# An attention and MLP kernel whose whole schedule is a printed list: the list replaced, with VectorE's squares and statistics kept apart from GpSimd's array reads

## The chip, the cores and the metric

The kernel runs on one core of a Trainium2 chip. The metric is the device time of one execution in microseconds; the time of the kernel before is the median of three runs. Beside these there is one profiled execution, with a record of every instruction: its time is 166.68 us, its span (first to last recorded instruction) 165.0 us.

## The reference, cut to what matters

Sparse attention over 4 batches of 8 heads (768 tokens, head size 64), each query seeing the 8 first tokens and its 96 last ones, with a bias that grows with distance; then, on the 3072 tokens of width 512, a projection to 1024, a SoLU with a layer norm, and a projection back.

```python
scores = scale * np.matmul(q, k.transpose(0, 1, 3, 2)) + bias
scores = np.where(keep, scores, -1000000000.0)     # 8 global tokens, 96 local ones
a = softmax(scores)
x = np.matmul(a, v)                                # (B, H, S, D) -> (B*S, H*D)
h = x @ w_in
solu = h * softmax(h)
mu = np.mean(solu, axis=-1, keepdims=True)
var = np.mean((solu - mu) ** 2, axis=-1, keepdims=True)
out = ((solu - mu) / np.sqrt(var + 1e-06) * g_ln) @ w_out
```

## The kernel before

All work is cut into 1116 steps; 762 of them issue something or hold a buffer and stand in a list, the others are landings of transfers and releases of buffers. A step is a handful of instructions on one engine. The kernel builds the steps in a fixed order (so each has a number), and then emits them in the order of the list `ORDER`. `SLOTS` says which buffer each step takes, `ENGS` which engine runs a step that could run on several, and `WARM` where matmuls on a constant (L1215) are put in between, only to keep TensorE at work. Each engine runs its steps in the order of the list and waits, at each, for what that step needs; a step that waits holds up everything behind it on its engine. SP is the queue that issues nearly all transfers, and it too goes strictly by the list: a load whose buffer isn't free yet holds up the loads behind it.

The steps of one batch b, with its head pairs p = 0 to 3:

- loads of q and k (384 KB each, into 7 buffers x32), a cast to 16 bits with a reordering (L271, L273, L275, on ScalarE, VectorE or GpSimd), 6 transposes on TensorE (L712) and a copy out of PSUM ("evac", L271 or L273). For batch 0 v comes in parts of 96 and 64 KB, later in parts of 192 and 160 KB, into 3 buffers v32, and is cast by any of the three.
- on GpSimd four small products on k for the global tokens (kg, L515); on TensorE the scores in two groups of columns for each pair (L839, L854), and the global scores (L910, L916); on ScalarE their exponentials (L862, L923). For batches 1 to 3 VectorE multiplies a factor on (fac, L871), which makes the bias; its table fb is made at the start (L314, L320).
- in two units u of 384 tokens: row sums on TensorE (L937, L946), their logarithm on ScalarE (L953), a split of it into a high part (lhi, L960, one buffer) and a rest (l16, a subtraction, L968) on VectorE or GpSimd, a spreading to all rows on TensorE (L997), the reciprocal as an exponential on ScalarE (L1006), probabilities times v on TensorE (av1, av2, L1031, L1041, with a one-column copy, "tick", L1051, between them), and their product on VectorE (xT, L1066).
- for each of 24 tiles t of 128 tokens: the first projection (gemm1, L1104; for tiles 0 to 5 in two halves), its exponential with row sums on ScalarE (ef, L1114), the product on VectorE (u, L1117, which frees the projection's pair of PSUM banks), the square with its row sum on ScalarE (L1124) or VectorE (L1128), a transposition by the DMA engines (tiles 5 to 21, issued by SP, L1133, into the buffer "late") or by TensorE (L1143), the output matmul (gemm2, L1189), its scaling (osb, L1199 on ScalarE, L1202 on VectorE) and the store (L1206).
- for each group of three tiles, four instructions on VectorE that make the variance from the row sums (stats, L1160 to L1167; groups are numbered 0 to 7), and two on ScalarE for its inverse root (L1171, L1172).

Once, at the start: constants on GpSimd and VectorE, among them iota (L297 to L301), the identity and a scaled identity (L289, L290), the bias (L338), and the slopes (L370); w_in and w_out, each as four loads of 512 KB; eight casts of w_in (four for each half of the columns); a mean over w_out (L626 part_mean, a copy on ScalarE, L631) and its centring on VectorE (L634, 8 steps), which the output matmul needs.

A step is given a mark `port` if its name begins with one of the names in `PORT`. The mark isn't read anywhere in the kernel.

Of the kernel before, what the change touches and what calls it, by code (L numbers as in the profile page):

```python
# [29 lines left out]
FACT = {1, 2, 3}  # L30
SPLIT = False
ORDER = """
# [32 lines left out]
"""  # L65
SLOTS = """
# [11 lines left out]
"""  # L78
ENGS = """
# [4 lines left out]
"""  # L84
WARM = """
28:0:4 34:0:1 44:4:1 51:4:1 78:2:4 97:6:2 113:4:3 120:4:2 145:2:3 173:6:1 199:5:1 203:4:1
"""


PORT = ("cast_", "w_in_cast", "c_far", "c_bias", "c_local", "c_rows", "fac", "lhi", "l16", "c_gbc",  # L90
        "c_spread", "c_sumg", "kg", "vgz")


class Plan:
# [1159 lines left out]
```

## Time and profile before

| | |
|---|---|
| median of 3 runs | 167.39 us (165.78 to 167.76) |
| profiled execution | 166.68 us, span 165.0 us |
| TensorE's granted clock | 1.00 in all stages |
| TensorE matmul instructions | 1955 |
| bytes moved by DMA | 34.26 MB, mean 208 GB/s |

The profile is read in five ways here. A table gives each engine's busy time over the span. A table by stretches gives the length, the busy time of TensorE's matmuls, of its weight loads, of VectorE (DVE), ScalarE (ACT) and GpSimd (POOL), each with the number of instructions, then the granted clock, the mean busy share of the 16 DMA engines, and GB/s. The timeline of an engine gives start, duration, engine, line, operation, output and input, and in brackets the idle time before it with what ended it; equal instructions in a row are merged (x5), and SPq is SP's issuing queue. A table of groups gives the instructions of one line with their total, their mean in ns, and the idle time before them. Names like acc (PSUM) or x are the program's tile names without buffer numbers.

### The profile page before, as it was taken

To read this page: it belongs to the slowest core of one execution; us is meant where nothing else is said; L and a number is where in the kernel's file an instruction comes from. 1 tells how busy PE (TensorE), PEld (TensorE's weight loads), DVE (VectorE), ACT (ScalarE), POOL (GpSimd) and SP (SyncE) were. 2 spreads that over 40 slices of the span, in tenths; PEclk is the share of its full clock that TensorE was granted. 3 is DMA by queue.
4 is the path that set the end of the run, shared out by engine and by line. 5 is a ranking of instruction groups with operands and counts; after the bars stand their busy time and mean duration, and the time that the engine had idled before them with its cause. 6 is when DMAs were issued, how large, how long until landed. Compare 5 with 4: busy or idle time off the path is not lost.

```text
span 165.0 us, 4929 instructions
## 1 busy us (share of the span) xinstructions
PE 148.6 (90%) x1955; PEld 82.1 (50%) x1955; DVE 128.1 (78%) x270; ACT 124.6 (76%) x206; POOL 52.3 (32%) x121
## 2 busy tenths in 40 slices
PE   4498976998998999989999999999997899997991
PEld 1366544345656655556555444574443464443650
DVE  6978334889987999989899999387979565569850
ACT  3566957659999999997999799787985752866612
POOL 7774515367166456443450610120041000000000
PEclk9999999999999999999999999999999999999999
DMA  4999699999999989899966449940672831359333
GB/s 153 372 346 258 159 321 359 392 339 275 293 299 301 292 224 228 231 285 336 297 111 133 100 92 264 265 171 0 131 120 72 189 124 71 71 128 123 124 134 126
DMA packets 58390, 34.26 MB, mean 208 GB/s; under 512 B 44920, under 2 KB 53376, under 8 KB 58368
## 3 DMA queue, kind: packets, MB, share of 16 engines
q1 hardware_dynamic: 57360, 32.26, 72.1%
q10 hardware_dynamic: 1008, 1.70, 3.0%
q8 instruction: 15, 0.25, 0.7%
q14 instruction: 7, 0.06, 0.1%
HBM read 23.20 MB, written 6.29 MB: 179 GB/s over the span
## 4 chain that ended last, share of the span: by engine, by line
PE 46%; DVE 18%; ACT 10%; DMA 8%; POOL 6%; issue 6%; SPq 2%; ACTq 0%; POOLq 0%; DVEq 0%
PE acc L1189 17%; PE acc L1104 10%; DVE uu L1117 6%; DMA v<-in_v_dram 5%; PE acc L1041 4%; PE acc L712 4%; ACT eb L862 3%; DMA late<-uu 3%; DVE gw_out_sb L634 2%; ACT ef L1114 2%; DVE eb L871 2%; DVE xT L1066 2%; PE acc L997 2%; DVE sqv L1128 2%; PE acc L1143 2%
## 5 line engine op out<-in xcount | busy, mean ns | idle before, releaser
L1189 PE MATMUL acc<-gw_out_sb,late 128*128 128x512 f16 (+1 forms) x200 | 44.7, 371 | 0.8 <-DMA late<-uu 0.8
L1104 PE MATMUL acc<-w_in_sb,xT 128*128 128x512 f16 x192 | 44.3, 379 | 0.5 <-DVE uu L1117 0.4
L1117 DVE SCALAR_TENSOR_TENSOR uu<-ef,acc 128x1024 f16<-128x1024 f16 x24 | 29.1, 1218 | 7.6 <-ACT ef L1114 7.3
L862 ACT ACTIVATE eb<-acc 128x960 f16<-128x960 f32 (+1 forms) x32 | 29.0, 949 | 4.9 <-PE acc L854 4.7
L1114 ACT ACTIVATE ef<-acc 128x1024 f16<-128x1024 f32 x24 | 24.7, 1030 | 9.7 <-PE acc L1104 9.6
L1189 PEld LDWEIGHTS <-late 128*128 128x128 f16 x200 | 18.6, 98 | 21.0 <-DMA late<-uu 1.3
L1104 PEld LDWEIGHTS <-xT 128*128 128x128 f16 x192 | 18.1, 98 | 21.8 <-issue 1.8
L1066 DVE TENSOR_TENSOR xT<-acc,rr 128x384 f16<-128x384 f32 x32 | 16.2, 551 | 4.5 <-PE acc L1041 2.4
L871 DVE TENSOR_TENSOR eb<-eb,fb 128x960 f16<-128x960 f16 x24 | 16.6, 697 | 3.3 <-ACT eb L862 3.1
L275 POOL CAST x<-x 128x768 f16<-128x768 f32 x17 | 15.6, 928 | 10.1 <-DMA x<-in_k_dram 3.1
L712 PE MATMUL acc<-ident,x 128*128 128x128 f16 x192 | 15.8, 231 | 2.9 <-ACT x L271 1.6
L712 PEld LDWEIGHTS <-x 128*128 128x128 f16 x192 | 12.7, 104 | 8.7 <-ACT x L271 2.9
L1006 ACT ACTIVATE rr<-acc 128x768 f32<-128x768 f32 x16 | 12.6, 809 | 5.3 <-PE acc L997 4.4
L1041 PE MATMUL acc<-eb,v 64*64 64x160 f16 (+4 forms) x448 | 14.8, 219 | 1.7 <-ACT lns L953 0.9
L1124 ACT ACTIVATE sqa<-uu 128x1024 f16<-128x1024 f16 x14 | 14.9, 1066 | 0.5 <-ACT osb L1199 0.4
L1041 PEld LDWEIGHTS <-v 64*64 64x64 f16 x448 | 12.6, 106 | 4.4 <-issue 2.9
L275 POOL CAST v<-v 128x704 f16<-128x704 f32 (+3 forms) x14 | 7.8, 582 | 21.0 <-DMA v<-in_v_dram 19.9
L1199 ACT ACTIVATE osb<-acc,rstd 128x512 f32<-128x512 f32 (+1 forms) x16 | 10.4, 672 | 4.4 <-PE acc L1189 4.1
L1128 DVE SCALAR_TENSOR_TENSOR sqv<-uu 128x1024 f16<-128x1024 f16 x10 | 12.6, 1260 | 0.1
L854 PE MATMUL acc<-qT,kT 64*64 64x160 f16 (+2 forms) x384 | 11.8, 230 | 0.5 <-ACT eb L862 0.5
L968 POOL TENSOR_TENSOR l<-lns,lhi 128x384 f16<-128x384 f32 x5 | 6.7, 1331 | 16.3 <-DVE lhi L960 15.6
L273 DVE COPY kT<-acc 128x768 f16<-128x768 f16 x11 | 10.5, 952 | 1.4 <-PE acc L712 1.4
(116 smaller groups left out, 206.3 us busy)
## 6 DMA issues: line engine op xcount, KB each, us to landing
x<-in_q_dram SPq DMA_DIRECT2D x16, 384.0 KB, 5.0
x<-in_k_dram SPq DMA_DIRECT2D x16, 384.0 KB, 6.4
out_dram<-osb SPq DMA_DIRECT2D x17, 256.0 KB, 4.0
v<-in_v_dram SPq DMA_DIRECT2D x12, 192.0 KB, 4.8
w_out<-in_moe_w_out_dram SPq DMA_DIRECT2D x4, 512.0 KB, 6.0
late<-in_moe_w_in_dram SPq DMA_DIRECT2D x4, 512.0 KB
v<-in_v_dram SPq DMA_DIRECT2D x12, 160.0 KB
out_dram<-osb ACTq DMA_DIRECT2D x6, 256.0 KB, 3.1
```

The source lines that it names most:

```text
L275: nc.gpsimd.tensor_copy(out=out, in_=in_)
L712: nc.tensor.transpose(out=pt[:, ts(j, P)], in_=a[:, j, ts(pp, P)], identity=ident)
L862: ex["fn"] = (lambda ex=ex, qk=qk, gw=gw: nc.scalar.activation(out=eb[at(qk, "eb")][:, :, 0:gw], in_=big(qk)[:, :, 0:gw], func=AF.Exp, sca ...
L871: nc.vector.tensor_tensor(out=e, in0=e, in1=bass.AP(tensor=f.tensor, offset=f.offset, ap=[f.ap[0], f.ap[1], [0, 3], f.ap[2]]), op=ALU.mult)
L1041: nc.tensor.matmul(out=o_[64 * h : 64 * h + 64, gl : gl + m], lhsT=vv[r, v_at(vi, h, c), pair, :], rhs=view(eb[at(e_own[b, gi, pair], "eb" ...
L1066: nc.vector.tensor_tensor(out=xT[at(xt_own[b], "xT")][:, p, q0:q1], in0=one(av, d)[:, 0:w], in1=rr[at(re, "rr")][:, d, 0:w], op=ALU.mult)
L1104: nc.tensor.matmul(out=ph()[:, ts(fh, 512)], lhsT=xT[at(xt_own[b], "xT")][:, j, ts(t % NA, P)], rhs=w_in_sb[:, j, ts(fh, 512)], start=(j = ...
L1114: ex["fn"] = lambda g1=g1, t=t, ph=ph: nc.scalar.activation(out=ef[at(g1, "ef")], in_=ph(), func=AF.Exp, accum_out=s0[:, t : t + 1])
L1117: u["fn"] = lambda u=u, g1=g1, t=t, ph=ph: nc.vector.scalar_tensor_tensor(out=uu[at(u, "uu")], in0=ef[at(g1, "ef")], scalar=USC, in1=ph(), ...
L1124: nc.scalar.activation(out=sqs_["ACT"], in_=uu[at(u, "uu")], func=AF.Square, accum_out=s2[:, t : t + 1])
L1128: nc.vector.scalar_tensor_tensor(out=sqs_["DVE"], in0=uu[at(u, "uu")], scalar=1.0, in1=uu[at(u, "uu")], op0=ALU.mult, op1=ALU.mult, accum_ ...
L1189: nc.tensor.matmul(out=one(g2)[:, 0:wd], lhsT=uT[at(el_o, "uT")][:, c, :], rhs=gw_out_sb[:, c, sl_], start=(c == 0), stop=(c == NFC - 1))
```

## The change

`PORT` gets two more names, and `ORDER`, `SLOTS`, `ENGS` and `WARM` are replaced. The functions, the shapes and the arithmetic are the same, and so are the steps: the new list holds the same 762.

```diff
 ORDER = """
-11 12 2 99 139 281 65 295 5 112 13 92 0 328 10 3 79 16 15 19 73 14 17 101 4 128 9 105 102 297 130
-6 103 24 298 1 86 18 7 20 22 94 133 23 95 66 21 299 114 96 8 115 123 330 183 116 81 45 331 184 75
...
+11 12 6 112 65 139 609 1 118 2 86 105 19 13 66 99 10 7 92 16 114 79 24 17 5 14 123 15 22 133 0 20
+23 88 73 3 115 21 4 29 89 107 116 18 108 45 109 101 163 185 90 9 94 157 213 68 186 102 8 120 214
...
 """
 SLOTS = """
...
 """
 ENGS = """
...
 """
 WARM = """
-28:0:4 34:0:1 44:4:1 51:4:1 78:2:4 97:6:2 113:4:3 120:4:2 145:2:3 173:6:1 199:5:1 203:4:1
+28:0:5 36:4:0 49:4:1 73:0:2 92:0:4 107:6:2 128:6:5 168:4:1 197:4:1 297:4:1
 """
 PORT = ("cast_", "w_in_cast", "c_far", "c_bias", "c_local", "c_rows", "fac", "lhi", "l16", "c_gbc",
-        "c_spread", "c_sumg", "kg", "vgz")
+        "c_spread", "c_sumg", "kg", "vgz", "sq", "stats")
```

The third number of each entry in `WARM` is the count of the constant matmuls: 24 before, 22 after. 94 steps get another engine: among them 40 casts of q, k, v and w_in, 14 copies out of PSUM of q and k, 10 squares (5 each way; 14 on ScalarE and 10 on VectorE as before), 9 output scalings (6 to VectorE, 3 to ScalarE), and 10 issues of stores.

Read out engine by engine, with the names above (q0.2 is q of batch 0, pair 2; t2 is tile 2; v5 the sixth of the v loads; two v loads make one pair of heads), the parts of the lists that are spoken of below are these.

SP, from its first issue to the last of w_in:

```text
before  q0.2 k1.1 q0.3 k0.2 q1.3 k0.1 q0.0 v4 k0.3 v5 q0.1 v6 k0.0 v2 glob v7 glob v3 v8 ends ends
        q1.1 w_out v0 v1 glob ends w_out g w_out w_out w_in w_in w_in w_in
after   q0.3 v0 q0.1 k0.3 k0.0 q0.2 k0.2 k0.1 v2 v6 q0.0 ends glob w_out w_out v1 g v3 k1.1 w_in
        glob ends v7 q1.1 v4 v5 w_out w_out w_in glob w_in w_in
```

("glob" and "ends" are small loads of v, 16 and 64 KB; g is 4 KB.) In the new list v4 takes the v32 buffer of v0 and v1.

ScalarE, from its start to the last cast of w_in:

```text
before  table, cast q0.2 k1.1 k0.2, factor 1 0, evac k0.2, exp, cast v, exp, evac q0.0, exp, cast v,
        exp exp exp exp exp, global exp 0 1, cast v (of v0, v1), ln 0, exp exp (batch 1), ln 1,
        reciprocal 0 1, copy of the mean, reciprocal 2 3, cast w_in
after   table, cast q0.3, factor 1 0, evac q0.3 k0.3, cast q0.2 k0.2, exp exp, evac k0.2 k0.1,
        exp exp exp exp, cast v (of v2, v3), global exp 1, exp, global exp 0, exp, cast w_in, ln 0, ln 1,
        cast q1.1, reciprocal 1 0, exp exp (batch 1), cast w_in, copy of the mean, reciprocal 2 3, cast w_in
```

GpSimd's constants, and its list to the first v cast of the new list:

```text
before  iota, small (L363 to L366), identity, onesq, pick, tails, spread, slopes, ident8, scaled identity, sums, ...
after   slopes, scaled identity, iota, tails, onesq, sums, ident8, small, identity, pick, spread,
        cast k0.0, sums_g, cast k0.1 q0.0, kg0.0 kg0.2 kg0.1 kg0.3, cast v (of v0, v1), vgz, ...
```

TensorE, from the row sums of batch 3, and VectorE beside it:

```text
before  sums 1 0, gemm1 t12 t13, gemm2 t16 t17, spread, spread, av2, gemm2 t14 ...
  DVE   u t16, u t15, lhi 0, sq t15, lhi 1, stats 5, u t12, sq t12, u t13, xT ...
after   sums 0, gemm1 t12 t13, av1, sums 1, spread, av2, gemm2 t14, gemm1 t17, gemm2 t12 ...
  DVE   u t14, u t15, lhi 0, sq t15, fac, u t12, tick, u t13, sq t13, lhi 1, xT, stats 4, xT ...
```

TensorE at the end:

```text
before  gemm1 t18 t21, gemm2 t13, gemm1 t19 t20, gemm2 t18, gemm1 t23 t22, gemm2 t19, turn t23,
        gemm2 t20, turn t22, gemm2 t23b t21 t22 t23
after   gemm1 t18 t22, gemm2 t15, gemm1 t21 t19, gemm2 t18, gemm1 t20, gemm2 t16, gemm1 t23, gemm2 t21,
        turn t22, gemm2 t19 t20, turn t23, gemm2 t22 t23b t23
```

90 rows, old and new, of tables (ENGS, ORDER, SLOTS) are left out of this document.

## The prediction

> **What bounds the kernel now.** I read the busy table first, then the stages, then the queues at the start.
>
> ```profile
> PE 148.6 (90%) x1955; PEld 82.1 (50%) x1955; DVE 128.1 (78%) x270; ACT 124.6 (76%) x206; POOL 52.3 (32%) x121
> ```
> ```profile
> 0.00:33.60 33.60, 26.22 (x409) 14.74 (x410) 21.91 (x59) 21.38 (x30) 17.25 (x71) 1.00 0.93 297
> 33.60:77.40 43.80, 41.30 (x673) 25.53 (x671) 40.93 (x78) 40.03 (x65) 22.29 (x38) 1.00 0.99 280
> 77.40:125.00 47.60, 46.99 (x590) 24.41 (x587) 41.24 (x82) 42.29 (x73) 12.81 (x14) 1.00 0.67 153
> 125.00:161.40 36.40, 34.08 (x290) 17.39 (x288) 24.02 (x53) 20.47 (x40) 0.00 (x0) 1.00 0.49 120
> 161.40:165.00 3.60, 0.04 (x1) 0.00 (x0) 0.00 (x0) 0.47 (x1) 0.00 (x0) 1.00 0.30 109
> ```
>
> TensorE (first column behind the length) carries 90% of the span. I cut the stages at the first projection matmul, at the projections of batch 1 and near the last softmax work. Idle TensorE time is 7.4 us in the start, 2.5, 0.6 and 2.3 us in the three stages behind it, and 3.6 us at the end. TensorE's work is the same in both kernels: 196 steps, no matmul added or dropped but two of the 24 warm-up matmuls. So the change can only move idle time, and the largest piece lies before 33.6 us. There ScalarE and VectorE are busy 21 to 22 of 33.6 us, so it is not their load that binds but waits. In the second stage VectorE (40.93) and ScalarE (40.03 of 43.80) are nearly full and the DMA engines are full (0.99): there a new order has little to gain and something to lose.
>
> What the start waits for is in ScalarE's and SP's queues:
>
> ```profile
> 17.73 4.31 ACT L862 ACTIVATE eb<-acc 128x960 f16<-128x960 f32 x5
> 21.89 1.09 ACT L923 ACTIVATE eg<-acc,gbias 128x384 f16<-128x384 f32 x2
> 25.10 0.51 ACT L271 CAST v<-v 128x384 f16<-128x384 f32 x1 [2.12 <-DMA v<-in_v_dram]
> 25.52 0.48 ACT L953 ACTIVATE lns<-acc 128x384 f32<-128x384 f32 x1
> ```
> ```profile
> 14.40 2.58 SPq L493 DMA_DIRECT2D vt<-in_v_dram  x2
> 18.25 0.94 SPq L485 DMA_DIRECT2D v<-in_v_dram  x2
> 23.47 3.12 SPq L602 DMA_DIRECT2D late<-in_moe_w_in_dram  x4
> ```
> ```profile
> 16.00:20.00 4.00, 4.00 (x108) 2.44 (x108) 1.92 (x2) 3.48 (x5) 2.07 (x6) 1.00 0.57 118
> 20.00:24.00 4.00, 2.99 (x55) 1.49 (x51) 1.52 (x2) 2.98 (x5) 0.00 (x0) 1.00 1.05 320
> ```
> ```profile
> 33.61 3.62 PE L1104 MATMUL acc<-w_in_sb,xT 128*128 128x512 f16 x16
> 34.77 0.61 POOL L275 CAST w_in_sb<-late 128x512 f16<-128x512 f32 x1 [0.18 <-DMA late<-in_moe_w_in_dram]
> ```
>
> A cast of v stands on ScalarE ahead of the logarithm (L953). Its load was issued at 18.25, and ScalarE stood 2.12 us until it landed. From 16 to 20 us the DMA engines moved 118 GB/s, against 320 just behind: SP was issuing a run of small loads. The last eighth of w_in landed at about 34.77, and the second half of every first projection needs it.
>
> **Part by part: the start.** First, the new list makes the very beginning later.
>
> ```profile
> 6.95 0.33 POOL L370 MEMSET slr<- 128x1 f32 x8
> 7.78 0.29 POOL L290 TENSOR_SCALAR_AFFINE_SELECT identb<-identb 128x128 f16<-128x128 f16 x1
> 3.98 1.92 DVE L338 TENSOR_SCALAR bw<-dm,sl 128x160 f16<-128x160 f32 x4
> 8.12 0.75 PE L314 MATMUL acc<-bw,identb 64*64 64x160 f16 x16 [1.20 <-POOL identb L290]
> 8.94 1.30 ACT L320 ACTIVATE fb<-acc 128x640 f16<-128x640 f32 x2 [0.35 <-PE acc L314]
> ```
>
> GpSimd now makes the slope row (0.33) and the scaled identity (a memset and the select of 0.29, together about 0.5) ahead of the iota, so the iota, VectorE's bias (end 5.90) and what follows come 0.8 us later: bias at 6.7, the bias matmuls (0.75, no longer waiting for identb) until 7.4, ScalarE's two factor exponentials (1.30) until 8.8. The plain identity moves from third to ninth among GpSimd's constants, so the first transposes come later too; but ScalarE's factor exponentials, which stand ahead of the first copy on its queue, end later still, so this costs nothing more.
>
> From 8.8 ScalarE's list to the logarithm holds 8 score exponentials (4.31 for five, so 6.9), 4 copies and 2 casts, one v cast (0.51), 2 exponentials of the global scores (1.09) and one cast of w_in.
>
> ```profile
> 41.45 0.81 ACT L271 COPY qT<-acc 128x768 f16<-128x768 f16 x1
> 4.15 0.83 ACT L271 CAST x<-x 128x768 f16<-128x768 f32 x1 [2.08 <-DMA x<-in_q_dram]
> 34.74 0.62 ACT L271 CAST w_in_sb<-late 128x512 f16<-128x512 f32 x1 [0.73 <-DMA late<-in_moe_w_in_dram]
> 32.49 1.52 ACT L1006 ACTIVATE rr<-acc 128x768 f32<-128x768 f32 x2
> 32.01 0.58 ACT L271 COPY part<-acc 128x512 f32<-128x512 f32 x1 [1.06 <-PE acc L626]
> ```
>
> That is 6.9 + 3.2 + 1.7 + 0.5 + 1.1 + 0.6 = 14.0, so the logarithm comes at 22.8 instead of 25.5, if ScalarE never waits: the v that it casts is now issued ninth and eighteenth on SP, not twenty-fourth and -fifth. Behind it until its last w_in cast stand two logarithms (0.9), a q cast (0.8), four reciprocals (3.0), two exponentials (1.7), two w_in casts (1.2) and the copy for the mean (0.6): 8.2, so 31.0. The loads agree. By the sizes told above (384 KB for each q or k, 512 KB for each quarter of w_in and w_out, 96 KB and less for the rest), 9.21 MiB stood on SP up to the last of w_in, and now 8.68: 0.56 MB, 1.7 us at 320 GB/s. The 118 GB/s hole lost (320 - 118) / 320 x 4 = 2.5 us; in the new list large loads stand between the small ones, and I take the hole as closed. 34.8 - 4.2 = 30.6, and a cast of 0.6: 31.2.
>
> So the second halves of the projections start at 31.2, not 35.4 (34.77 + 0.61); of the 3.62 us block one quarter lies ahead of them, and it ends at 33.9 instead of 37.2. One transpose of batch 1 (0.34) now lies behind it. **Start: -3.0.** Bounds: -4.2 (the loads alone) and -0.5 (the hole stays, and SP waits once more).
>
> **The middle, 34 to 77 us.**
>
> ```profile
> L1199 ACT ACTIVATE osb<-acc,rstd 128x512 f32<-128x512 f32 (+1 forms) x16 | 10.4, 672 | 4.4 <-PE acc L1189 4.1
> L1202 DVE TENSOR_SCALAR osb<-acc,rstd 128x512 f32<-128x512 f32 (+1 forms) x9 | 6.4, 717 | 1.8 <-ACT rstd L1172 1.0 <-PE acc L1189 0.6
> ```
>
> From the first projection's exponential to the first reciprocal of batch 1, ScalarE has 42 steps for 45: four output scalings fewer (0.67 each) and one cast more (0.83), so -1.9. VectorE, from the first centring of w_out to the first product of batch 1, has 56 for 54: two output scalings more (0.72 each), and among the copies and casts as many come as go; I take +1.8 as an estimate. Both are full, and both feed the same matmuls. **Middle: 0**, between -1.9 and +1.8.
>
> **The named aim: squares and statistics away from GpSimd.**
>
> ```profile
> 59.43 1.61 DVE L1128 SCALAR_TENSOR_TENSOR sqv<-uu 128x1024 f16<-128x1024 f16 x1
> 94.76 0.87 DVE L1160 SCALAR_TENSOR_TENSOR va<-s 128x3 f32<-128x3 f32 x1
> 123.65 0.90 DVE L1163 SCALAR_TENSOR_TENSOR va<-s,va 128x3 f32<-128x3 f32 x1
> 126.00 1.23 DVE L1128 SCALAR_TENSOR_TENSOR sqv<-uu 128x1024 f16<-128x1024 f16 x1
> 151.75 0.16 DVE L1160 SCALAR_TENSOR_TENSOR va<-s 128x3 f32<-128x3 f32 x1
> 93.80 1.81 POOL L968 TENSOR_TENSOR l<-lns,lhi 128x384 f16<-128x384 f32 x1
> 29.48 0.91 POOL L968 TENSOR_TENSOR l<-lns,lhi 128x384 f16<-128x384 f32 x1 [2.13 <-DVE lhi L960]
> ```
>
> One square took 1.61 instead of 1.23, and two statistics steps 0.87 and 0.90 instead of 0.16: 1.8 us in all. [...] But most of the 1.8 us is not on TensorE's path. What reached it is here:
>
> ```profile
> 95.67 0.36 PE L997 MATMUL acc<-l,onesr 64*64 64x384 f16 x4 [0.41 <-DVE va L1160]
> 128.43 0.36 PE L997 MATMUL acc<-l,onesr 64*64 64x384 f16 x4 [1.49 <-DVE uu L1117]
> 151.72 1.90 PE L1189 MATMUL acc<-gw_out_sb,late 128*128 128x512 f16 x8 [0.83 <-DMA late<-uu]
> ```
>
> The first is the 0.87. The second waits for a PSUM pair that the product of tile 13 frees; ahead of that product VectorE had a split, a statistics group with the 0.90 in it, the product of tile 12 and a square. The new list has the products of tiles 12 and 13 together, with only a one-column copy between, the square and the rest behind: 1.23 + 0.90 = 2.1 us sooner, so this wait goes. The third is a transposed tile that landed late: between the projection of tile 19 and its output matmul lay three projections and one output block (1.8 us each, half of the 3.62 above); now it is two projections, three output blocks and a transpose, 1.8 us and more beyond, against 0.83. **Late: -2.7 for these.** Against them I put 1.2 us of new waits, half of what the middle shows in a similar length. Net -1.5, bounds -2.7 and +1.5. The end itself (last block, scaling, store) keeps its length.
>
> Sum: -3.0 + 0 - 1.5 = -4.5. The profiled execution took 166.68 us for its span of 165.0; it would be 162.2. The median of the three runs, 167.39, lies 0.7 above it, so I forecast 162.9.
>
> **The rivals.** *The middle eats the lead.* VectorE was busy 93.4% of the middle; at that share its 1.8 us more cost 1.9, and the late waits may come back in other places (1.2): 162.9 + 3.1 = 166.0. For it: two full engines and a full DMA. Against it: ScalarE's list is shorter by about as much, and 16.38 MiB instead of 16.93 stand on SP up to the last q or k of batch 2, so the loads don't hold it.
>
> *The separation is only on paper.* The lists hold no time: what runs beside what is left to the chip. In the new list the square of tile 15 still stands right behind the split that releases GpSimd's subtraction, as before, so at least this pair still meets; there it is covered by two projections. If the statistics meet GpSimd on the path too, 0.71 and 0.74 come back: 162.9 + 1.45 = 164.4. [...]
>
> *Slower: SP stuck behind one v load.* The fifth v load of batch 0 needs the buffer of the first, which GpSimd frees with a cast that now stands behind four small products on k.
>
> ```profile
> 18.99 0.74 POOL L515 TENSOR_TENSOR kg<-kT,hpick 128x16 f16<-128x16 f16 x4 [0.81 <-DVE kT L273]
> ```
>
> Behind that load on SP stand two quarters of w_out and three of w_in. Seven issues (0.5 each) and 8.2 us from SP's last w_in issue (26.6) to landing (34.8) make 11.7, so if the cast ends later than about 23 us, w_in lands later than before, one for one. I expect 16 to 17; before, the products ended at 19.7. At 23 the start's 3.0 is gone (165.9), at 28.5 the time is 171.4.
>
> **Chances.** Forecast 0.58, the middle 0.22, on paper 0.09, SP past 27.8 us 0.08; 0.03 for slower in ways I don't see. The range reaches from most of the gains at their bounds (162.9 - 1.2 - 1.2 - 1.0 = 159.5) to a start at its worse bound with 2.4 us of late or middle loss (162.9 + 2.5 + 2.4 = 167.8). 2% of 167.39 is 3.3 us, about what this kernel's runs (165.78 to 167.76) can tell from nothing: below 164.0 lie 0.54 of the forecast's 0.58 and 0.03 of the second rival, 0.57; above 170.7 SP's and the unseen, 0.11; 0.32 between.
>
> **What would show it.** Right: the first L953 near 23 without a DMA wait, the first L1104 near 30, no hole in GB/s at 16 to 20, TensorE at 128 us without a wait for VectorE, the L1160 and L1163 rows at 0.16. Wrong: w_in landing past 33 us, new TensorE idle time between 34 and 110 us of more than 3 us, or GpSimd's subtraction again at 1.8 with TensorE waiting for it.

## The result and the profile after

The new list takes 162.31 us (median of 4 runs, 161.68 to 162.93), the old one 167.39 beside it: a ratio of 0.9715, 95% interval 0.9636 to 0.9794, so 3.4 to 6.1 us less (ratios are of undisturbed executions alone, medians of all). The profiled execution took 162.93 us, the slowest of the four, its span 161.1.

The busy table of the kernel after, and then the table by stretches, with its columns as before:

```profile
PE 150.1 (93%) x1953; PEld 82.7 (51%) x1953; DVE 130.4 (81%) x271; ACT 123.0 (76%) x206; POOL 52.4 (33%) x120
```
```profile
0.00:33.60 33.60, 28.13 (x411) 15.97 (x412) 22.73 (x61) 25.49 (x37) 17.65 (x70) 1.00 0.97 303
33.60:77.40 43.80, 42.43 (x689) 25.86 (x688) 42.74 (x79) 40.41 (x66) 24.14 (x36) 1.00 1.04 297
77.40:125.00 47.60, 46.83 (x594) 24.12 (x592) 41.45 (x82) 38.73 (x69) 10.66 (x14) 1.00 0.63 136
125.00:157.60 32.60, 32.60 (x264) 16.72 (x262) 23.51 (x53) 17.94 (x36) 0.00 (x0) 1.00 0.54 126
```

TensorE's idle time, the first column of us less the second, was 7.4, 2.5, 0.6, 2.3 and 3.6 us; it is 5.5, 1.4, 0.8, 0.0 and (161.1 - 157.6 - 0.15 of work) 3.35. Idle time fell by 5.4 us in all, TensorE's busy time rose by 1.5 (148.6 to 150.1), and the span fell by 3.9. From 125 to 157.6 us TensorE no longer waits at all. In the second stage VectorE is busy 42.74 and TensorE 42.43 of 43.80 us: both are nearly full there.

The start, in the kernel after: ScalarE from its first score exponential, TensorE's first projections, and two stretches of 4 us.

```profile
12.28 1.77 ACT L862 ACTIVATE eb<-acc 128x960 f16<-128x960 f32 x2
13.94 1.50 ACT L271 COPY kT<-acc 128x768 f16<-128x768 f16 x2
15.42 3.45 ACT L862 ACTIVATE eb<-acc 128x960 f16<-128x960 f32 x4
18.73 0.53 ACT L271 CAST v<-v 128x384 f16<-128x384 f32 x1
...
22.23 1.05 ACT L953 ACTIVATE lns<-acc 128x384 f32<-128x384 f32 x2
...
32.09 0.62 ACT L271 CAST w_in_sb<-late 128x512 f16<-128x512 f32 x1 [0.74 <-DMA late<-in_moe_w_in_dram]
```
```profile
31.23 3.88 PE L1104 MATMUL acc<-w_in_sb,xT 128*128 128x512 f16 x16
```
```profile
16.00:20.00 4.00, 3.65 (x80) 2.06 (x69) 1.95 (x4) 4.00 (x7) 1.05 (x5) 1.00 0.98 291
20.00:24.00 4.00, 3.50 (x61) 1.80 (x59) 3.11 (x6) 3.98 (x7) 1.69 (x2) 1.00 1.02 276
```

No bracket stands behind any ScalarE row from 12.28 to the logarithm at 22.23: the queue ran through, and the wait for v is gone. The hole of 118 GB/s is closed (291). The last of w_in landed at 32.1, 2.7 us sooner than the 34.77 of before.

The squares and statistics did not stay apart from GpSimd. In the kernel after, GpSimd's row first and VectorE's beside it, then the other squares and statistics steps that took longer than usual:

```profile
114.82 1.82 POOL L968 TENSOR_TENSOR l<-lns,lhi 128x384 f16<-128x384 f32 x1 [12.30 <-DVE lhi L960]
```
```profile
114.66 1.22 DVE L1128 SCALAR_TENSOR_TENSOR sqv<-uu 128x1024 f16<-128x1024 f16 x1
115.80 0.08 DVE L1128 DVE_READ_ACCUMULATOR sqv<-uu 128x1 f32 x1
115.80 1.36 DVE L871 TENSOR_TENSOR eb<-eb,fb 128x960 f16<-128x960 f16 x1
```
```profile
38.83 1.61 DVE L1128 SCALAR_TENSOR_TENSOR sqv<-uu 128x1024 f16<-128x1024 f16 x1
64.91 1.78 DVE L1128 SCALAR_TENSOR_TENSOR sqv<-uu 128x1024 f16<-128x1024 f16 x1
90.95 0.84 DVE L1163 SCALAR_TENSOR_TENSOR va<-s,va 128x3 f32<-128x3 f32 x1
91.89 0.62 DVE L1167 TENSOR_TENSOR va<-va,vb 128x3 f32<-128x3 f32 x1
```

It is the same pair as before: the subtraction begins just behind the start of the square of tile 15 and takes 1.82 instead of 0.91 us. And the factor behind the square took 1.36 instead of 0.65. The other four rows stand beside casts of GpSimd (38.54 to 39.36, 64.67 to 65.61, 91.72 to 92.50) or, the third, beside a subtraction of it (90.86 to 91.77). A square usually takes 1.22, a statistics step 0.16; so squares and statistics lost 0.39 + 0.56 + 0.68 + 0.46 = 2.1 us here, and 1.8 before. There was no less meeting than before.

A second measure is used below: how much sooner (-) or later a kernel had done the same part of TensorE's work than the kernel before. The first row is the end of the first block of projections. There all kernels have done the same matmuls, but for one step of six transposes (0.34 us), which the new list has behind it and which is allowed for, and for the constant ones. For the other rows each matmul counts with the mean TensorE time of its kind (line and shape) in the trace of before behind 15 us, the constant ones left out. Another weighting moves single values of the new order by up to 0.4 us, but hardly the differences among 10, 9, 11 and after. The left columns are the share and the time in the kernel before; 5, 6, 9, 10, 11 are experiments told below.

```
share   before    after     5      6      9     10     11
block    37.22    -1.78  -0.55  +0.25  -1.27  +1.88  -1.56
 45%     82.28    -1.94  -0.66  -0.45  -2.09  -0.08  -2.78
 69%    117.23    -2.12  -0.66  -0.45  -2.26  -0.26  -2.95
 85%    140.33    -2.77  -1.50  -1.02  -3.14  -0.90  -3.59
 97%    156.95    -3.77  -2.50  -1.25  -4.05  -1.83  -4.55
```

The new list is 1.8 us ahead at the end of the first block, 1.9 at 82 us, 2.1 at 117, 3.8 near the end.

### The profile page after: what moved, and what is told of

Read it like the earlier page. It is cut to its first block, busy times and chain, and to the rows that moved or that the text cites. A ratio compares the mean times of both kernels' runs of the same rounds, so it can differ in the third digit from the quotient of the medians.

```text
span 161.1 us, 4916 instructions
## 1 busy us (share of the span) xinstructions
PE 150.1 (93%) x1953; PEld 82.7 (51%) x1953; DVE 130.4 (81%) x271; ACT 123.0 (76%) x206; POOL 52.4 (33%) x120
## 4 chain that ended last, share of the span: by engine, by line
PE 50%; DVE 20%; DMA 13%; SPq 5%; issue 5%; ACT 3%; POOL 1%; DVEq 0%; ACTq 0%
PE acc L1189 24%; PE acc L1104 13%; DMA late<-in_moe_w_in_dram 9%; DMA x<-in_q_dram 5%; DVE eb L871 4%; DVE uu L1117 4%; DVE xT L1066 3%; PE acc L712 3%; PE acc L1041 3%; SPq L471 3%; DVE qT L273 2%; PE acc L854 2%; DVE v L273 1%; DVE sqv L1128 1%; ACT ef L1114 1%
## 5 line engine op out<-in xcount | busy, mean ns | idle before, releaser
L1117 DVE SCALAR_TENSOR_TENSOR uu<-ef,acc 128x1024 f16<-128x1024 f16 x24 | 29.1, 1214 | 8.6 <-ACT ef L1114 8.5
L275 POOL CAST x<-x 128x768 f16<-128x768 f32 x20 | 18.1, 918 | 14.8 <-DMA x<-in_k_dram 6.1
L871 DVE TENSOR_TENSOR eb<-eb,fb 128x960 f16<-128x960 f16 x24 | 17.9, 761 | 0.6 <-ACT eb L862 0.5
L712 PEld LDWEIGHTS <-x 128*128 128x128 f16 x192 | 13.2, 107 | 7.0 <-issue 2.1
L275 POOL CAST v<-v 128x704 f16<-128x704 f32 (+3 forms) x14 | 9.1, 651 | 13.8 <-DMA v<-in_v_dram 13.8
L1199 ACT ACTIVATE osb<-acc,rstd 128x512 f32<-128x512 f32 (+1 forms) x13 | 8.4, 659 | 6.6 <-PE acc L1189 5.9
L273 DVE COPY qT<-acc 128x768 f16<-128x768 f16 x11 | 10.4, 949 | 3.7 <-PE acc L712 3.7
L1128 DVE SCALAR_TENSOR_TENSOR sqv<-uu 128x1024 f16<-128x1024 f16 x10 | 13.2, 1316 | 0.2
L854 PE MATMUL acc<-qT,kT 64*64 64x160 f16 (+2 forms) x384 | 13.1, 234 | 0.0
L1031 PE MATMUL acc<-eg,vgz 64*64 64x384 f16 x64 | 10.4, 324 | 0.0
```

Source lines behind the costliest of these rows:

```text
L273: nc.vector.tensor_copy(out=out, in_=in_)
L275: nc.gpsimd.tensor_copy(out=out, in_=in_)
L712: nc.tensor.transpose(out=pt[:, ts(j, P)], in_=a[:, j, ts(pp, P)], identity=ident)
L854: nc.tensor.matmul(out=sc[o : o + 64, par, col : col + n], lhsT=kk[r, BLK * c : BLK * c + BLK], rhs=qq[r, g0 : g0 + n], start=fresh, stop= ...
L871: nc.vector.tensor_tensor(out=e, in0=e, in1=bass.AP(tensor=f.tensor, offset=f.offset, ap=[f.ap[0], f.ap[1], [0, 3], f.ap[2]]), op=ALU.mult)
L1117: u["fn"] = lambda u=u, g1=g1, t=t, ph=ph: nc.vector.scalar_tensor_tensor(out=uu[at(u, "uu")], in0=ef[at(g1, "ef")], scalar=USC, in1=ph(), ...
```

## The experiments

Three theories stood against each other. The gain lies in the start (loads and ScalarE's queue) and in the late waits; or in the late part alone, the middle eating the start's lead; or in the separation of VectorE from GpSimd. In runs 1 to 4 line numbers are one lower than in the other kernels. All ratios are against the kernel before on the same chip (medians 166.6 to 166.8).

**Runs 1 to 4: one part of the new list, the rest of the old, and the other way round.** Buffers were given anew where the old choice was taken.

```diff
 ORDER, run 1 (run 2 the other way round)
-old list
+new list to the second half of tile 0's projection (191 steps), then what is left of the old list
 ORDER, run 3 (run 4 the other way round)
-old list
+old list to the projection of tile 15 (630 steps), then what is left of the new list
```

> The new list up to the first projections (the second half of tile 0's), then the old order for all the rest, with buffers given anew where the old choice is taken and two early loads for batches 2 and 3 in the old place. If the start's gain is real and lasts (theory): the first block of projections ended at 35.1 us in the new kernel and at 37.2 in the old one, so 167.4 - 2.1 = 165.3. If the middle, whose two engines are full, eats the lead (rival): 167.4, with the first block still ending near 35.

> The counterpart: the old list up to the first projections (without one early load of batch 3), then the new order. Theory: 162.3 + 2.1 = 164.4. Rival (the gain was made behind the start): 162.3.

> The old list up to the projection of tile 15 (about 118 us), then the new order for the rest. Theory: TensorE's idle time behind 125 us goes from 2.3 us to nearly none, so 167.4 - 2.2 = 165.2. If the late waits come back elsewhere (rival): 167.4. If what counts is that squares and statistics are apart from GpSimd (second rival), the time moves only as far as the 0.90 us statistics step at about 123.65 goes: 166.5.

> The new list up to the projection of tile 15, then the old order. Theory: 162.3 + 2.2 = 164.5, with TensorE waiting again for VectorE near the end of batch 3's attention. Rival (no late effect): 162.3. Second rival (statistics beside GpSimd): 163.2.

Measured: 173.75 us (ratio 1.0426, 1.0355 to 1.0497), 172.33 (1.0294, 1.0207 to 1.0381), 173.59 (1.0401, 1.033 to 1.0471) and 166.77 (0.9997, 0.9956 to 1.0038). No theory foresaw this: three of the four times lie above both parents, and run 4's is that of the kernel before. Run 1, TensorE's timeline, SP's, and stretches of 2 us:

```profile
30.86 3.63 PE L1103 MATMUL acc<-w_in_sb,xT 128*128 128x512 f16 x16
38.51 1.46 PE L711 MATMUL acc<-ident,x 128*128 128x128 f16 x12 [4.03 <-DVE x L272]
```
```profile
34.49 0.64 SPq L492 DMA_DIRECT2D vt<-in_v_dram  x1
38.48 0.37 SPq L470 DMA_DIRECT2D x<-in_q_dram  x1
```
```profile
38.00:40.00 2.00, 1.46 (x12) 1.30 (x13) 1.08 (x2) 0.00 (x0) 0.61 (x1) 0.50 0.15 23
44.00:46.00 2.00, 2.00 (x9) 0.96 (x8) 2.00 (x4) 0.62 (x2) 1.12 (x2) 0.50 1.05 359
48.00:50.00 2.00, 2.00 (x17) 1.13 (x15) 0.27 (x1) 1.72 (x4) 0.29 (x1) 1.00 1.08 349
```

The start itself did what was expected: the block of first projections ended at 30.86 + 3.63 = 34.5, against 37.2 before. But at the seam a load of q stood on SP for a buffer that was not free until 38.48 (3.4 us behind the issue ahead of it), with all loads behind it; TensorE waited 4.03 us for a cast, and then ran at a granted clock of 0.50 to 48 us. In run 2 TensorE waited 5.24 us for a cast at its seam, in run 3 3.62 us for a product on VectorE; in run 4 it waited four times for products between 117 and 131 us, 0.58 to 1.38 us each. So these four tell nothing of what start and tail are worth apart: a list's parts fit each other by their buffers, and a seam cost as much as a lead or more.

**Run 8: run 1 with the seam mended.**

```diff
 ORDER, around the seam
-SP: ... q1.3, v, v, ends, q1.2 (into the buffer of q1.3) ...     TensorE: transposes of q1.3 first
+SP: ... q1.3, v, v, ends, q1.2 (into a free buffer) ...          TensorE: transposes of k1.2 k1.3 first
```

> The first of these runs again, new list to the first projections and old order behind, now with the two stalls at the seam taken out: the load of q that held SP for 3.4 us gets a buffer that is free, and the cast and transposes of batch 1's last q come later, as that load now does. Theory: the block ends near 34.5 us and the lead lasts: 166.7 - 2.5 = 164.2. Rival (the lead is lost in the full middle): 166.7 or more.

Measured: 168.60 us, ratio 1.0127 (1.0086 to 1.0168). Better than run 1 by 5 us, still slower than before: by its numbers the rival. But in its profile (of an execution of 170.35 us) the block of first projections ended at 37.3 us, not at 34.5 as in run 1: the lead that the middle was to eat was not there, so this run doesn't decide. Run 10 says more.

**Run 5: two late waits, by order alone.**

```diff
 VectorE
-... lhi 1, stats 5, u t12, sq t12, u t13, xT ...
+... lhi 1, u t12, u t13, stats 5, sq t12, xT ...
 TensorE, and ef, u, the square and the transposing DMA with it
-gemm1 t18 t21, gemm2 t13, gemm1 t19 t20 ...
+gemm1 t18 t19, gemm2 t13, gemm1 t21 t20 ...
```

> The old list with two places of its late part changed. VectorE takes the product of tile 13 straight behind that of tile 12, the statistics of group 5 and the square of tile 12 after both; and the projections of tiles 19 and 21 change places, with what hangs on them. Nothing is moved between VectorE and GpSimd. Theory (the late waits are TensorE's own path): the waits of 1.49 us for the product and of 0.83 us for the transposed tile go, so 2.3 us less than before: 166.7 - 2.3 = 164.4. Rival (they come back a few steps on): no change, 166.7.

Measured: 164.95 us, ratio 0.9923 (0.989 to 0.9956), so 1.3 us less (0.7 to 1.8). TensorE's timeline at the two places:

```profile
125.92 0.52 PE L997 MATMUL acc<-l,onesr 64*64 64x384 f16 x8
129.32 1.89 PE L1189 MATMUL acc<-gw_out_sb,late 128*128 128x512 f16 x8 [0.54 <-DVE xT L1066]
149.23 1.89 PE L1189 MATMUL acc<-gw_out_sb,late 128*128 128x512 f16 x8
```

Both waits are gone (no bracket at 125.92 and 149.23), and one of 0.54 has come back a few steps on. In the table of leads, 1.84 us were won behind 117 us. The order of a few VectorE steps and two tiles is worth this, while GpSimd's subtraction still took 1.82 us beside the square. One meeting did go by it: the statistics step that took 0.90 us before (123.65) takes 0.16 here (125.20). How much of the gain that is, no run tells apart.

**Run 6: the two subtractions of batch 3 off GpSimd, in the old list.**

```diff
 ENGS
-l16 of batch 3, units 0 and 1: GpSimd
+l16 of batch 3, units 0 and 1: VectorE
```

> The old list with the two subtractions of batch 3 on VectorE, not on GpSimd, so that behind 109 us GpSimd reads no array at all and cannot meet a square or statistics. If the meetings are what costs (the change's own reason, rival): VectorE no longer waits 0.80 us for GpSimd's subtraction and 0.74 us inside the statistics, TensorE's wait of 1.49 us goes altogether: 165.2. Theory (order decides): VectorE does 0.5 us twice itself and still has a square ahead of the product of tile 13, the product comes about 0.6 us sooner, and TensorE still waits some 0.8 us: 166.7 - 0.6 = 166.1.

Measured: 166.26 us, ratio 0.9958 (0.991 to 1.0005): 0.7 us less (-0.1 to 1.5). TensorE at the place:

```profile
127.41 0.36 PE L997 MATMUL acc<-l,onesr 64*64 64x384 f16 x4 [0.92 <-DVE uu L1117]
```

The wait fell from 1.49 to 0.92, by 0.6 as order foresaw; the rival's 165.2 (a ratio of 0.991) lies at the interval's edge, but the wait that it needed to lose entirely is there, if shorter. A part of the 1.49 was indeed the meeting (0.80 and 0.74 us of VectorE, less the subtractions it now did itself).

**Run 7: SP's first loads alone.**

```diff
 SP
-... v2 glob v7 glob v3 v8 ends ends q1.1 w_out v0 v1 glob ends w_out g w_out w_out w_in w_in w_in w_in ...
+... v2 glob v7 w_out v3 v0 v1 ends q1.1 w_out glob ends g w_out w_out w_in w_in w_in w_in glob v8 ends ...
```

> The old list with only SP's first loads put in another order: one quarter of w_out and the two loads of v0 and v1 come among the run of small loads, and three small loads that batch 0's first half does not need (one of v8, two for later batches) come behind w_in. Theory: no hole in GB/s between 16 and 20 us, ScalarE's logarithm without the 2.12 us wait, first block of projections ending 2 to 2.5 us sooner, and most of it kept: 166.7 - 2.0 = 164.7. Rival (middle eats it): block sooner, time 166.7. Rival (the loads were not what held the start; the chain of casts and exponentials was): block at 37 us as before, 166.7.

Measured: 166.66 us, ratio 0.9973 (0.9928 to 1.0018), no change that can be told. ScalarE, and the stretch that had the hole:

```profile
9.73 0.83 ACT L271 CAST x<-x 128x768 f16<-128x768 f32 x1 [3.78 <-DMA x<-in_k_dram]
...
24.39 0.57 ACT L271 CAST v<-v 128x384 f16<-128x384 f32 x1
24.80 0.56 ACT L953 ACTIVATE lns<-acc 128x384 f32<-128x384 f32 x1
```
```profile
16.00:20.00 4.00, 3.80 (x81) 2.27 (x80) 2.41 (x4) 2.77 (x5) 1.74 (x3) 1.00 0.91 230
```

The hole is nearly closed (230 against 118) and the wait for v is gone, yet the logarithm comes only 0.7 us sooner (25.52 before), within the 24.05 to 25.10 of the runs 2, 3, 5 and 6, whose start is that of before. In this profile a load of k landed 2 us later than in that of before, with the same issues ahead of it. The wait that this removes was also less than it looked: in runs 2, 3, 5 and 6 ScalarE waited 1.08, 1.30, 0.61 and 1.03 us there, not 2.12. The one profile of before showed the largest of five. The last of w_in landed at 33.9, the block of first projections ended 0.65 us sooner, and no gain can be told: closing the hole alone is not what makes the new start.

**Run 9: GpSimd's last two subtractions moved too, in the new kernel.**

```diff
 ENGS
-l16 of batch 2 unit 1 and batch 3 unit 0: GpSimd
+l16 of batch 2 unit 1 and batch 3 unit 0: VectorE
```

> The new list with its last two GpSimd subtractions (batches 2 and 3) moved to VectorE, so that no square or statistics step behind 88 us meets GpSimd reading an array. In the new kernel these meetings made one subtraction take 1.82 instead of 0.91 us and one statistics step 0.84 instead of 0.16, none of them with TensorE waiting. Theory (apart or not, only what is on TensorE's path counts): 162.3 as it is, between 161.8 and 162.8. Rival (the meetings cost what they last): 162.3 - 0.7 - 0.9 = 160.7.

Measured: 162.65 us, ratio 0.9691 (0.96 to 0.9782), beside 0.9715 of the new list as it is: no change. VectorE, where the factor had taken 1.36:

```profile
114.52 1.22 DVE L1128 SCALAR_TENSOR_TENSOR sqv<-uu 128x1024 f16<-128x1024 f16 x1
115.66 0.08 DVE L1128 DVE_READ_ACCUMULATOR sqv<-uu 128x1 f32 x1
115.66 0.65 DVE L871 TENSOR_TENSOR eb<-eb,fb 128x960 f16<-128x960 f16 x1
116.23 0.55 DVE L968 TENSOR_TENSOR l<-lns,lhi 128x384 f16<-128x384 f32 x1
```

The factor is at 0.65 again, and VectorE does the subtraction itself for 0.55. Meetings with GpSimd's casts are left (a square still took 1.40 us, at 39.73). The interval alone would just allow the rival's 160.7; the leads don't: from 117 us to the end this kernel gains 1.8 us, the new one 1.65.

**Run 10: the cast of the first v pair late.**

```diff
 GpSimd
-... kg0.0 kg0.2 kg0.1 kg0.3, cast v (of v0, v1), vgz, ...
+... kg0.0 kg0.2 kg0.1 kg0.3, vgz, cast v (of v0, v1), ...
```

> The new list with one thing put back: on GpSimd the cast of the first v pair comes behind the spreading of batch 0's global v (1.04 us, which waits for its own load until 21.6 us). The cast then ends at about 23 instead of 18.8, and SP's fifth v load, two quarters of w_out and three of w_in wait for it. If the prediction's rival priced it rightly, one for one: w_in lands some 4 us later, 162.3 + 3.5 = 165.8. If the DMA engines make it up, or the loads come early enough anyway: 162.3 to 163.5.

Measured: 166.01 us, ratio 0.9946 (0.9906 to 0.9987). GpSimd, SP, TensorE, and two stretches:

```profile
22.45 1.21 POOL L275 CAST v<-v 128x384 f16<-128x384 f32 x2
...
35.32 0.61 POOL L275 CAST w_in_sb<-late 128x512 f16<-128x512 f32 x1 [0.52 <-DMA late<-in_moe_w_in_dram]
```
```profile
23.18 0.90 SPq L485 DMA_DIRECT2D v<-in_v_dram  x2
24.13 0.99 SPq L613 DMA_DIRECT2D w_out<-in_moe_w_out_dram  x2
```
```profile
35.14 3.63 PE L1104 MATMUL acc<-w_in_sb,xT 128*128 128x512 f16 x16 [0.45 <-DVE w_in_sb L273]
```
```profile
20.00:24.00 4.00, 3.42 (x61) 1.73 (x59) 3.23 (x6) 3.11 (x6) 2.20 (x3) 1.00 0.56 148
28.00:32.00 4.00, 4.00 (x72) 2.16 (x64) 1.74 (x4) 1.89 (x2) 1.33 (x2) 0.69 0.95 300
```

One step moved on GpSimd put off the fifth v load on SP from 19.16 to 23.18, the hole opened again (148 GB/s), w_in landed 3.2 us later, the first projections began 3.9 us later, and the time went up: by 3.7 us in the medians, by 2.0 in the two profiled executions (164.94 and 162.93). The block of first projections ended 3.7 us later than in the new kernel, 1.9 later than in that of before; at 82 us and at the end this kernel is 1.9 us behind the new one. So in these profiles the middle made up about half of the loss, and the rest came through to the end. The timing of SP's queue is needed for the start's gain, and the middle doesn't eat all of it. What the rest of the new list is worth can't be read from the remaining 0.5% (0.1 to 0.9), since this start is worse than that of before; by the leads, it won 1.75 us behind 82 us (-0.08 to -1.83).

**Runs 11 and 12: can the start be better still?**

```diff
 run 11 (run 12 too)
-ScalarE: ... evac k0.2 k0.1 ... cast v (of v2, v3) ... cast w_in, ln 0, ln 1 ...    GpSimd: identity ninth
+ScalarE: ... evac k0.2 ... ln 0, ln 1, cast w_in ...                               GpSimd: identity fourth
+VectorE: evac k0.1      GpSimd: cast v (of v2, v3)
 run 12
-SP: v2 v6 q0.0 ends glob w_out w_out v1 g v3 k1.1 w_in glob ends v7 q1.1 v4 v5 ...
+SP: q0.0 v2 v6 v1 ends glob w_out w_out g v3 glob ends v7 k1.1 w_in v4 v5 q1.1 ...
```

> The new list, ScalarE relieved ahead of the first logarithm: one copy (0.75 us) to VectorE and one v cast (0.4) to GpSimd, which are idle there, the first cast of w_in (0.5) behind the second logarithm; the plain identity is made right behind the iota on GpSimd. If ScalarE's list sets the start: the logarithm comes 1 to 1.6 us sooner and the time is 162.3 - 1.0 = 161.3. If loads set it (the fifth v load landed at 24.6, the last quarter of w_in at 32.1): 162.3, with the idle time only moved.

> The same, and SP's first loads in another order: the last q of batch 0, the second half of the first v pair and the fifth v load earlier, one k and one q of batch 1 and a small load later, and the first halves of the first two projections ahead of both second halves. If ScalarE's list and the loads set the start together: 162.3 - 1.5 = 160.8. If neither does (TensorE is busy from 24 us on): 162.3.

Measured: 162.15 us, ratio 0.9695 (0.963 to 0.9761), and 165.20, ratio 0.9872 (0.9804 to 0.994). In run 11 ScalarE had 1.65 us less ahead of the logarithm, which came at 21.85 instead of 22.23:

```profile
21.85 0.49 ACT L953 ACTIVATE lns<-acc 128x384 f32<-128x384 f32 x1
23.11 0.49 ACT L953 ACTIVATE lns<-acc 128x384 f32<-128x384 f32 x1 [0.77 <-PE acc L946]
```

The time saved turned into waits, as here, and TensorE's first projections began at 31.70, 0.5 us later than in the new kernel's own profile. So a shorter ScalarE list alone does not make the new start better; that it and the loads are about level would explain this, but was not shown. Run 12's new order of loads made it worse (first projections at 33.33); which of its moves did, was not tried. No version beats the new list by more than its measurement tells.

## Why the prediction was right, step by step

**What bounds the kernel.** Idle TensorE time was read as the only thing that could move, with its largest piece in the start. Idle time did give the gain, but busy time moved too, by +1.5 us. Some 0.4 of that is one more constant matmul ahead of 4 us. Some 1.1 (an estimate, half of 2.16 us) comes from a slower pace: transposes started every 107 ns until 14.0 us here, until 11.8 before, and every 56 ns behind that. The table prints a granted clock of 1.00 for this stretch, but the trace's first record of the clock stands only at 14.00 here and at 11.84 before. Run 10 shows how much hangs on the start: with SP's queue put off, 3.7 us of the medians' gain (0.9946 against 0.9715, so 2.3% with some 0.9% either way) was lost, and 2.0 of the profiled pair's.

**Start, -3.0 forecast.** The lead at the end of the first block is 1.8 us in the profiled pair and 1.3 in run 9, whose start is the same. The direction holds, and the path through v, SP's queue and w_in; the term was 1.2 to 1.7 us too large, and its inner steps hold less well. *"The new list makes the very beginning later"*, with the bias at 6.7 us, was wrong: VectorE's bias took 0.97 us instead of the 1.92 of before, and its matmuls ran at 4.01.

```profile
3.64 0.97 DVE L338 TENSOR_SCALAR bw<-dm,sl 128x160 f16<-128x160 f32 x4
```
```profile
4.01 1.14 PE L314 MATMUL acc<-bw,identb 64*64 64x160 f16 x16 [0.19 <-DVE bw L338]
6.69 1.44 PE L712 MATMUL acc<-ident,x 128*128 128x128 f16 x12 [1.54 <-POOL pick L342]
11.80 2.54 PE L712 MATMUL acc<-ident,x 128*128 128x128 f16 x24
```

Why the bias is twice as fast was not tried. The late identity did hold the first transposes (to 6.69, 1.54 us of waiting). It was not covered as forecast, since ScalarE had ended its factor exponentials at 6.07, not at 8.8, and waited 1.46 us for these transposes. It cost nothing all the same: in run 11, with the identity fourth and the first transposes at 5.76, the first score exponential came at 12.24, here at 12.28. *"6.9 + 3.2 + 1.7 + 0.5 + 1.1 + 0.6 = 14.0"* from 8.8 on, without a wait, was wrong twice: ScalarE came to this list 2.7 us sooner, waited 3.0 us in it ahead of 12.28 (1.46 and 1.31 for transposes, 0.27 for a load), and its work was some 13.1 us. The errors nearly cancel, so that the logarithm, forecast at 22.8, came at 22.23; that is in part luck. *"I take the hole as closed"* was right, but 320 GB/s behind it was too much: 291 and 276. So w_in landed at 32.1, not 30.6, the block began at 31.23, not about 30, and ended at 35.1, not 33.9; that is the part of the 3.0 us that is missing. Which of the new list's moves makes the start sooner stays partly open: run 10 shows that v must free its buffer in time, run 7 that a nearly closed hole in the old list is not enough. And a price was read from one profile: the wait of 2.12 us varied between 0.61 and 2.12.

**Middle, 0 forecast.** From the first block to 117 us the lead went from 1.8 to 2.1 us in the profiled pair, and from 1.3 to 2.3 in run 9. That is -0.3 and -1.0, inside the bounds of -1.9 and +1.8. The rival that the middle eats the lead doesn't fit: the lead is there at 117 us, and in run 10 only half of a start put off was made up.

**Late, -1.5 forecast.** Of the three named waits, -2.7, the 1.49 and the 0.83 went; the 0.41 was only changed for another (0.39 us for a copy, at 93.44), and one of 0.37 for a product came at 118.35. Run 5 took away the same two, 2.3 us, and gained 1.3 by the ratio, 1.84 in the leads: 1.0 or 0.5 came back, where the forecast put 1.2. In the leads the new list gains 1.65 us behind 117 us, run 9 1.8. This term holds.

**The separation.** *"The separation is only on paper"* described what happened, down to the named pair, but its price of 1.45 us did not come. TensorE waited 0.37 us at 118.35 for the product that stood behind the lengthened factor. But in run 9, with the factor at 0.65 and the subtraction on VectorE, it waited 0.39 there, so no price of this meeting by itself is shown. The statistics rows of L1160 are at 0.16 as forecast, L1163 has one at 0.84 and L1167 one at 0.62, so that sign was half right. The gain can't come from the separation, since squares and statistics lost no less to GpSimd than before. To move GpSimd's late subtractions was worth 0.7 us (-0.1 to 1.5) in the old kernel and nothing that can be told in the new one.

**SP stuck behind one v load.** This did not come (the cast ended at 18.8; I had expected 16 to 17), for another reason than forecast: it waited 1.72 us for its own load, not for the products on k. Its price came near: with the cast's end at about 23 us the prediction gave 165.9, and run 10's median is 166.01; its profiled execution took 164.94, so the close agreement is in part chance.

**The sum.** -3.0 + 0 - 1.5 gave 162.2 for the profiled execution, which took 162.93, and 162.9 for the median, which is 162.31. The leads of the profiled pair give -1.8 - 0.3 - 1.65 = -3.75, just the difference of the two profiled executions; the medians differ by 5.1. So the start was put too large, middle and late a little too small, and that 162.9 lies so near the measured median is in part luck.

## What to carry to other kernels

In a kernel whose engines run fixed queues, price a new order by the waits that end last in each stage, and look in the start for the one buffer for which the load queue stands still: moving one cast of 0.5 us on an engine with idle time cost 3.7 us in the medians, 2.0 in the profiled executions. A list of this kind is one piece; a part of it put into another list can cost more than the whole gains. That a conflict lengthens instructions says little of its price: here 2.1 us were lost to it, and moving the late ones of them away brought nothing that could be told in the new kernel.

## What the runs showed of the hardware

**Some instructions of GpSimd and VectorE took turns, whole.** In the rows of the kernel after, GpSimd's subtraction issued at 114.82 ends at 116.64, 0.84 us behind the end of the square's work at 115.80 (where it comes first, at 90.86, it takes 0.91); the factor queued at 115.80 then ends at 117.16, 0.52 behind (alone, in run 9, it takes 0.65). The square, which came first, is not lengthened, and each of the others ends a little less than its own length behind the one ahead of it, so it looks as if it waits for that to end. The squares at 38.83 and 64.91, which came second, both end 1.08 us behind the end of GpSimd's cast (39.36 to 40.44, 65.61 to 66.69). So in these rows a meeting costs whoever comes second, and can be handed on. Not all instructions took part: VectorE's products (L1117), which read one operand from PSUM, took 1.20 to 1.22 us beside GpSimd's casts too (at 58.97, for one).

**A long wait of TensorE was paid again in runs 1 to 3.** In run 3:

```profile
128.70 0.54 PE L996 MATMUL acc<-l,onesr 64*64 64x384 f16 x4 [3.62 <-DVE uu L1116]
```
```profile
130.00:132.00 2.00, 2.00 (x6) 0.63 (x5) 1.34 (x7) 0.48 (x2) 0.00 (x0) 0.50 0.64 120
136.00:138.00 2.00, 2.00 (x20) 0.83 (x20) 0.02 (x1) 1.84 (x3) 0.00 (x0) 1.00 0.34 129
```

With a wait of 3.62 us the granted clock stood at 0.50 from 127.47 to 134.29 in run 3, and in run 1, with waits of 4.03 and 2.38, from 37.70 to 47.94: 6.8 and 10.2 us. In run 2, with a wait of 5.24, it was 3.4 us. At 0.50 the work went at about half speed: in run 1 eight transposes (L1142) took 1.06 us at 45.50, and 0.61 at 48.33, with the clock at 1.00 again. Run 3 did some 5.6 us of work so, run 1 some 7, and by an estimate from these the lower clock cost some 3 us beyond the wait. Waits and clock together (6.4 us in run 3, 9.9 in run 1 less the 2.7 that its start was ahead) are about the 7 us by which both came out slower than before. In run 10 the clock was at 0.50 from 27.04 to 30.45, after two waits of 1.56 and 0.57 us close together. How long a wait this takes was not shown: in run 3 the clock fell 2.4 us into the wait, in run 1 3.2 us; a wait of 1.49 us in the kernel before (at 128.43) left it at 1.00; and run 10 suggests that it need not be one unbroken wait.
